# Holding back one load of V until the rows of the group before are scaled, with one attention schedule moved by a step

## The chip, the cores and the metric

The kernel runs on one core of a Trainium2 chip. The metric is device time in microseconds (us) of one launch. Engines are named as in the profile: PE (TensorE matmul), PEld (its weight loads), DVE (VectorE), ACT (ScalarE), POOL (GpSimd) and SP (SyncE, which issues transfers here).

## The reference

Linear attention without softmax, a root-mean-square norm on each head's rows, and then two dense products with an ELU between them:

```python
kv  = einsum('bhsd,bhse->bhde', k, v)            # q, k, v: (8, 8, 576, 64)
out = einsum('bhsd,bhde->bhse', q, kv)
rms = sqrt(mean(out * out, axis=-1) + 1e-06)
x   = (out / rms * g_norm)                        # as 4608 x 512
h   = x @ w_in                                    # 512 x 2048
g   = where(h > 0, h, exp(min(h, 0)) - 1)
y   = g @ w_out                                   # 2048 x 512, float32
```

## The kernel before, in words

**Groups.** The 4608 rows of x are worked on in nine groups T = 0 to 8 of 512 rows. A group is eight slots of 64 rows; a batch has nine such slots (`slot_of`), so that group T needs the attention of batches T - 1 and T, or of one of them. For each group PE makes the first product (`mm1`: eight tile pairs i = 0 to 7, 128 x 512 each half, contracted over four chunks c of x) and the second (`mm2_half`: four column blocks of rows, each in two halves of eight matmuls). The order of all instructions on every engine is the order in which the Python program emits them[...].

**ELU.** `elu` takes exp on ACT from PSUM (L350), then DVE makes min(e, 1) - 1 (L362) and the maximum or sum with h (L366). With `relu` set, ACT also writes Relu of h (L355), which frees the PSUM pair, and DVE adds from SBUF; tiles 3 and 5 of group 2 are made so.

**Attention of a group** (`attention`, names used in the schedule): `kv` multiplies K and V of the group's new batch (L156) and ACT copies the result to SBUF (L268). `se0` and `se1` make the rows of the two halves of the group (L250), each followed by a square on ACT (L277). `sum` sums the squares on DVE (L283), `inv` makes one over the root on ACT (L291, L292), and `mul` scales the rows into `xs` on DVE (L299) and has SP issue two DMA transposes of them into `xT` (L306). `gain` multiplies the transposed columns of that half by g_norm on DVE (L312). `kv`, `se0` and `se1` share one PSUM tile, `at`, so that each waits until the one before has been read: `se1` waits for `mul0`.

**Loads.** Q, K and V come by DMAs that POOL issues, K and V cast to bf16 on the way (L90). Q arrives in float32, POOL casts it (L103), and SP transposes it by DMA into `qT` (`turn_q`, L331). `after_turn` has POOL copy 16 elements of `qT` (L339), so that POOL's next loads are issued after that transpose has landed; `fetch_ahead(b)` then issues Q, K and V of batch b.

**Order around the change.** Ahead of the groups' code, POOL's program has the loads of batch 2, its casts, `after_turn(2)`, `fetch_ahead(3)` and the casts of batch 3. Group 1's first product then carries the attention of group 2 in it: `se0` and `se1`, `mul0` (first two L306) and `mul1` (other two). The second product of group 1 on two row blocks follows, then `gain0` and `gain1`, and group 2's first product begins: tile pair 0 is made in two halves of columns, 0:256 after `gain0`, 256:512 after `gain1`.

In groups 2 to 7 `window` runs over the eight tile pairs: after pair i's matmuls it emits `early[i]`, a half of the second product of group T - 1 if there is one for i, the ELU's DVE part, and `late[i]`. The pieces are those of the attention of group T + 1. Group 2's lists are:

```python
early = {2: ("sum0", "inv0"), 5: ("sum1", "inv1", "mul1"), 6: ("gain0",), 7: ("gain1",)}
late = {0: ("kv",), 1: ("se0",), 2: ("mul0",), 4: ("se1",), 5: ("ahead",)}
halves = {1: 5, 3: 6, 5: 7}
```

**Group 0** is made chunk by chunk as the loads come in. `early(tiles, c)` (L569) adds chunk c to the listed tiles (i, a) of the first three pairs; chunks come in the order 0, 2, 1, 3. Pair 0's PSUM is taken again by pair 4 of the same group, which thus waits for the ELU of pair 0.

Of the kernel before, what the change touches and what calls it, by code (L numbers as in the profile page):

```python
# [9 lines left out]
BF16 = mybir.dt.bfloat16  # L10
# [6 lines left out]
def kernel(  # L17
# [13 lines left out]
    nc = tc.nc  # L31
# [6 lines left out]
    J = 4  # L38
# [6 lines left out]
    const = ctx.enter_context(tc.tile_pool(name="const", bufs=1))  # L45
# [35 lines left out]
    def fetch(name, b, u=None):  # L81

        if (name, b) not in bf:
            bf[name, b] = qkvp.tile([P, 4, RK, D], BF16, name=f"{name}_bf", tag=name)
        ms = slice(0, 4) if u is None else slice(u, 4, 2)
        load(bf[name, b][:, ms], name, b, ms)

    def load(dst, name, b, ms=slice(0, 4), eng=nc.gpsimd):
        in_ = src_of[name][b].rearrange("h r d -> (h r d)").rearrange("(m p x) -> p m x", m=4, p=P)
        eng.dma_start(out=dst.rearrange("p m j d -> p m (j d)"), in_=in_[:, ms, :])  # L90

    def fetch_ahead(b):
        raw[b] = stage.tile([P, 4, RK, D], FP32, name="st_q", tag="q")
        load(raw[b], "q", b)
        for name in "kv":
            fetch(name, b)

    def cast_q(b):
# [27 lines left out]
    def at_tile():  # L126
        return ps_at.tile([P, 2, 512], FP32, name="at", tag="at")
# [19 lines left out]
    def x_tile(T):  # L147
        xT[T] = attp.tile([P, KC, G], BF16, name="xT", tag="xT")
        return xT[T]

    def kv_mm(b, kv_ps, u, ls=range(2)):
        for j in range(RK):
            for s in range(2):
                rows = slice(s * 64, s * 64 + 64)
                for l in ls:
                    nc.tensor.matmul(  # L156
                        kv_ps[s][l * 64 : l * 64 + 64, u * 64 : u * 64 + 64],
                        lhsT=bf["k", b][rows, 2 * l + u, j, :],
                        rhs=bf["v", b][rows, 2 * l + u, j, :],
                        start=(j == 0),  # L160
                        stop=(j == RK - 1),
                    )
# [78 lines left out]
    def se_mm(T, h, se_ps):  # L241

        for i in range(2):
            (b0, j0), (b1, j1) = (slot_of(T, 4 * h + 2 * i + t) for t in range(2))
            parts = [(0, P, b0, j0, 2)] if b0 == b1 else [(0, 64, b0, j0, 1), (64, P, b1, j1, 1)]
            for m in range(4):
                u, s = m // 2, m % 2
                for l in range(2):
                    for lo, hi, b, j, n in parts:
                        nc.tensor.matmul(  # L250
                            se_ps[lo:hi, l, (4 * i + m) * 64 : (4 * i + m) * 64 + 64],
                            lhsT=qT[b][l * 64 : l * 64 + 64, s, u, j : j + n, :],
                            rhs=kv_of(b, l, u, s),
                            start=True,
                            stop=True,
                        )

    def attention(T):

        st = {}  # L260

        def kv():
            if T == B:
                return
            kv_ps = at_tile()
            for u in range(2):
                kv_mm(T, [kv_ps[:, s, :] for s in range(2)], u)
            nc.scalar.copy(  # L268
                kv_sb[:, T], kv_ps[:, :, 0:P].rearrange("p s (u e) -> p u s e", u=2)
            )  # L270

        def se(h):
            def product():
                st["se", h] = at_tile()
                se_mm(T, h, st["se", h])
                sq = attp.tile([P, 2, DM], BF16, name="sq", tag="sq")
                nc.scalar.activation(sq, st["se", h], AF.Square)  # L277
                st["sq", h] = sq

            def sums():  # L280
                ss = attp.tile([P, 2 * H], FP32, name="ss", tag="ss")
                st["ss", h] = ss
                nc.vector.reduce_sum(  # L283
                    out=ss,
                    in_=st.pop(("sq", h)).rearrange("p l (m e) -> p (l m) e", e=D),
                    axis=AX.X,
                )

            def inv():
                ss = st["ss", h]  # L290
                nc.scalar.activation(ss, ss, AF.Ln, bias=eps_col, scale=1.0 / D)  # L291
                nc.scalar.activation(ss, ss, AF.Exp, scale=-0.5)  # L292

            def scale():
                if h == 0:
                    st["xs"] = attp.tile([P, J, DM], BF16, name="xs", tag="xs")
                    x_tile(T)
                se_ps, ss = st.pop(("se", h)), st.pop(("ss", h))
                nc.vector.tensor_tensor(  # L299
                    out=st["xs"][:, 2 * h : 2 * h + 2, :].rearrange("p i (l m e) -> p l i m e", l=2, e=D),  # L300
                    in0=se_ps.rearrange("p l (i m e) -> p l i m e", i=2, e=D),
                    in1=ss.rearrange("p (l i m) -> p l i m", l=2, i=2).unsqueeze(4).to_broadcast([P, 2, 2, 4, D]),
                    op=ALU.mult,
                )
                for i in (2 * h, 2 * h + 1):
                    nc.sync.dma_start_transpose(  # L306
                        out=xT[T][:, :, i * P : i * P + P], in_=st["xs"][:, i, :]
                    )

            def gain():  # L310
                cols = slice(2 * h * P, 2 * h * P + 2 * P)
                nc.vector.tensor_scalar(  # L312
                    out=xT[T][:, :, cols],
                    in0=xT[T][:, :, cols],
                    scalar1=g_col,
                    scalar2=None,
                    op0=ALU.mult,
                )

            return product, sums, inv, scale, gain  # L320

        pieces = {"kv": kv}
        for h in range(2):
            for name, piece in zip(("se", "sum", "inv", "mul", "gain"), se(h)):
                pieces[f"{name}{h}"] = piece
        return pieces
# [9 lines left out]
    def after_turn(b):  # L336

        gate = const.tile([1, 16], BF16, name="gate")
        nc.gpsimd.tensor_copy(out=gate, in_=qT[b][0:1, 0, 1, RK - 1, 0:16])  # L339
# [170 lines left out]
    cast_q(2)  # L510
    turn_q(2)
    after_turn(2)
    fetch_ahead(3)
    cast_q(3)

    nc.vector.memset(zeros, 0.0)
# [48 lines left out]
    def early(tiles, c):  # L565

        for i, a in tiles:
            h = h_ps[i]
            nc.tensor.matmul(  # L569
                h[a] if isinstance(h, list) else h[:, a, :],  # L570
                lhsT=w_in_sb[:, c, (2 * i + a) * P : (2 * i + a) * P + P],
                rhs=xT[0][:, c, :],
                start=(c == 0),
                stop=(c == KC - 1),
            )
# [66 lines left out]
    early([(0, 0), (0, 1), (1, 0), (1, 1), (2, 0)], 1)  # L642
    h_ps[2][1] = single("m", "h_ps")
    early([(2, 1)], 0)
    early([(2, 1)], 2)
    early([(0, 0), (0, 1)], 3)
    early([(2, 1)], 1)
    early([(1, 0), (1, 1), (2, 0), (2, 1)], 3)
    for i in range(3):
# [53 lines left out]
    at = attention(2)  # L703
# [23 lines left out]
    at["sum1"]()  # L727
    at["inv1"]()
    at["mul1"]()
    for i in (6, 7):  # L730
        freed[i]()
    for i in (6, 7):
# [35 lines left out]
    for T in range(2, NT):  # L768
        at, early, late = {}, {}, {}
        if T + 1 < NT:  # L770
            at = attention(T + 1)
            if T + 2 < B:
                cast_q(T + 2)

                def ahead(b=T + 2):
                    turn_q(b)
                    if b + 1 < B:
                        after_turn(b)
                        fetch_ahead(b + 1)
                at["ahead"] = ahead  # L780
            else:
                at["ahead"] = lambda: None
            early = {2: ("sum0", "inv0"), 4: ("sum1", "inv1"), 5: ("gain0",), 7: ("gain1",)}
            late = {0: ("kv",), 1: ("se0",), 2: ("mul0",), 3: ("se1",), 4: ("mul1", "ahead")}
        if T == 2:
            early = {2: ("sum0", "inv0"), 5: ("sum1", "inv1", "mul1"), 6: ("gain0",), 7: ("gain1",)}
            late = {0: ("kv",), 1: ("se0",), 2: ("mul0",), 4: ("se1",), 5: ("ahead",)}
        halves = {1: 5, 3: 6, 5: 7} if T == 2 else {0: 1, 1: 3, 2: 4, 3: 5, 4: 6, 5: 7}
        second = {i: (lambda n=n: mm2_half(T - 1, n)) for i, n in halves.items()}
        if T > 2:  # L790
            window(T, at, early, late, second)
        else:
            g_tile(T)
            opened = [pair("B", "h_ps")]
            mm1_part(T, 0, opened[0], range(KC), slice(0, 256))
            window(T, at, early, late, second, (3, 5), opened)
        mm2_half(T, 0)
        mm2_half(T, 2)
# [33 lines left out]
```

## Time and profile before

| | before |
|---|---|
| device time, three runs | 285.09, 285.09, 286.17 us; median 285.09 |
| the profiled execution | 286.17 us, of which its span is 284.4 |
| PE busy | 276.9 us, 97% of the span, 2123 matmuls |
| DVE, ACT, POOL busy | 58%, 50%, 17% |
| granted TensorE clock | 1.0 throughout |
| L306, transposes of the rows | 28, median 2.5 us to landing, longest 9.1 |
| L90, loads of V of a whole batch | 6, median 12.6 us to landing |

Spans and starts are in us from the first instruction of the profiled execution. A busy PE is not a PE at its peak: the ends of matmuls are modelled, and holes are better read from the distances between the starts. "Idle before, releaser" in a line is the time for which that engine stood still and what ended it. A DMA's line shows its issue; when its data has arrived is the time to landing.

### The profile page before, as it was taken

To read this page: it belongs to the slowest core of one execution; us is meant where nothing else is said; L and a number is where in the kernel's file an instruction comes from. 1 tells how busy PE (TensorE), PEld (TensorE's weight loads), DVE (VectorE), ACT (ScalarE), POOL (GpSimd) and SP (SyncE) were. 2 spreads that over 40 slices of the span, in tenths; PEclk is the share of its full clock that TensorE was granted. 3 is DMA by queue.
4 is the path that set the end of the run, shared out by engine and by line. 5 is a ranking of instruction groups with operands and counts; after the bars stand their busy time and mean duration, and the time that the engine had idled before them with its cause. 6 is when DMAs were issued, how large, how long until landed. Compare 5 with 4: busy or idle time off the path is not lost.

```text
span 284.4 us, 5154 instructions
## 1 busy us (share of the span) xinstructions
PE 276.9 (97%) x2123; PEld 129.1 (45%) x2123; DVE 164.4 (58%) x222; ACT 141.4 (50%) x209; POOL 47.9 (17%) x89
## 2 busy tenths in 40 slices
PE   8899999999899999999999999999999999999994
PEld 3444444444544444444444444444444444444443
DVE  2549532966487657754785378627863786344600
ACT  3778359594468255435542555345543554333311
POOL 7743303303330033033003120000000000000000
PEclk9999999999999999999999999999999999999999
DMA  7999999999896889779627971612150234020222
GB/s 208 198 203 207 206 263 236 174 298 144 191 282 72 163 182 239 94 176 262 148 37 172 248 173 35 157 37 74 37 113 0 74 39 111 0 76 0 74 74 75
DMA packets 50571, 39.46 MB, mean 139 GB/s; under 512 B 30964, under 2 KB 44020, under 8 KB 50548
## 3 DMA queue, kind: packets, MB, share of 16 engines
q0 software_dynamic: 15008, 21.30, 37.4%
q1 hardware_dynamic: 35136, 17.31, 29.4%
q10 hardware_dynamic: 404, 0.53, 0.5%
q8 instruction: 16, 0.26, 0.3%
q14 instruction: 7, 0.06, 0.1%
HBM read 36.70 MB, written 9.44 MB: 162 GB/s over the span
## 4 chain that ended last, share of the span: by engine, by line
PE 87%; DMA 6%; DVE 2%; ACT 2%; POOL 1%; issue 0%; SPq 0%; DVEq 0%; POOLq 0%
PE h_ps L382 40%; PE o_ps L403 40%; DMA xT<-xs 3%; DMA v_bf<-in_v_dram 3%; PE at L250 2%; PE at L156 1%; PE o_ps L440 1%; PE h_ps L569 1%; ACT elu_e L350 1%; DVE gT L366 1%; POOL k_bf L90 1%; PE mean L199 0%; PE qt_ps L174 0%; PE kv_ps L156 0%; PE y_ps L189 0%; DVE ss L283 0%
## 5 line engine op out<-in xcount | busy, mean ns | idle before, releaser
L403 PE MATMUL o_ps<-w_out_sb,gT 128*128 128x512 bf16 x560 | 129.7, 379 | 0.0
L382 PE MATMUL h_ps<-xT,w_in_sb 128*128 128x512 bf16 (+1 forms) x560 | 128.0, 376 | 1.0 <-DVE xT L312 0.9
L350 ACT ACTIVATE elu_e<-h_ps 128x1024 bf16<-128x1024 f32 (+1 forms) x79 | 74.0, 952 | 90.6 <-PE h_ps L382 89.0
L403 PEld LDWEIGHTS <-gT 128*128 128x128 bf16 x560 | 54.4, 98 | 65.8 <-issue 0.9
L382 PEld LDWEIGHTS <-w_in_sb 128*128 128x128 bf16 x560 | 53.2, 98 | 62.4 <-PE o_ps L403 1.4
L366 DVE TENSOR_TENSOR gT<-elu_e,h_ps 128x1024 bf16<-128x1024 bf16 (+1 forms) x67 | 77.2, 1157 | 6.9 <-PE h_ps L382 0.5
L362 DVE TENSOR_SCALAR elu_e<-elu_e 128x1024 bf16<-128x1024 bf16 x72 | 31.2, 433 | 64.6 <-ACT elu_e L350 64.6
L419 ACT COPY o_sb<-o_ps 128x512 f32<-128x512 f32 x32 | 18.3, 587 | 21.1 <-PE o_ps L403 21.1
L103 POOL CAST q_bf<-st_q 128x384 bf16<-128x384 f32 x36 | 16.8, 508 | 41.6 <-DMA st_q<-in_q_dram 41.6
L283 DVE TENSOR_REDUCE ss<-sq 128x16 f32<-128x1024 bf16 x14 | 17.1, 1220 | 6.8 <-ACT sq L277 6.8
L299 DVE TENSOR_TENSOR xs<-at,ss 128x1024 bf16<-128x1024 f32 x14 | 17.1, 1219 | 1.9 <-ACT ss L292 1.9
L277 ACT ACTIVATE sq<-at 128x1024 bf16<-128x1024 f32 x14 | 14.4, 1029 | 0.0
L212 DVE SCALAR_TENSOR_TENSOR xT<-y_ps,g_col,rT 128x512 bf16<-128x512 f32 (+1 forms) x10 | 6.2, 641 | 10.1 <-ACT rT L209 7.9
L339 POOL COPY gate<-qT 1x16 bf16<-1x16 bf16 x5 | 1.1, 217 | 59.0 <-DMA qT<-q_bf 59.0
L355 ACT ACTIVATE elu_h<-h_ps 128x1024 bf16<-128x1024 f32 (+1 forms) x12 | 9.3, 817 | 0.0
L156 PEld LDWEIGHTS <-k_bf 64*64 64x64 bf16 x576 | 6.4, 107 | 5.5 <-issue 5.5
L312 DVE TENSOR_SCALAR xT<-xT,g_col 128x1024 bf16<-128x1024 bf16 x14 | 6.7, 480 | 3.3 <-DMA xT<-xs 3.3
L90 POOL DMA_DIRECT2D v_bf<-in_v_dram x11 | 7.7, 700 | 4.2 <-DMA w_in_sb<-in_moe_w_in_dram 2.1
L90 POOL DMA_DIRECT2D k_bf<-in_k_dram x11 | 7.7, 704 | 2.6 <-DMA w_in_sb<-in_moe_w_in_dram 1.8
L250 PEld LDWEIGHTS <-qT 64*128 64x128 bf16 (+1 forms) x248 | 4.3, 97 | 6.1 <-issue 5.9
L112 DVE COPY o_sb<-o_ps 128x256 f32<-128x256 f32 x1 | 0.4, 424 | 11.1 <-PE o_ps L440 11.1
L366 DVE TENSOR_TENSOR gT<-elu_e,elu_h 128x1024 bf16<-128x1024 bf16 x9 | 6.2, 692 | 0.8
(57 smaller groups left out, 101.3 us busy)
## 6 DMA issues: line engine op xcount, KB each, us to landing
st_q<-in_q_dram POOLq DMA_DIRECT2D x6, 1152.0 KB, 8.4
out_dram<-o_sb SPq DMA_DIRECT2D x24, 256.0 KB, 3.4
k_bf<-in_k_dram POOLq DMA_DIRECT2D x6, 576.0 KB, 10.5
v_bf<-in_v_dram POOLq DMA_DIRECT2D x6, 576.0 KB, 12.6
out_dram<-o_sb SPq DMA_DIRECT2D x19, 128.0 KB, 2.4
w_out_sb<-in_moe_w_out_dram POOLq DMA_DIRECT2D x4, 512.0 KB, 15.4
w_in_sb<-in_moe_w_in_dram POOLq DMA_DIRECT2D x2, 512.0 KB, 10.7
q_bf<-in_q_dram POOLq DMA_DIRECT2D x3, 288.0 KB, 13.4
```

Of the source, the lines that this page charges most:

```text
L90: eng.dma_start(out=dst.rearrange("p m j d -> p m (j d)"), in_=in_[:, ms, :])
L103: nc.gpsimd.tensor_copy(out=bf["q", b][:, u, js], in_=raw[b][:, u::2, js, :].rearrange("p l j d -> p j l d"),)
L250: nc.tensor.matmul(se_ps[lo:hi, l, (4 * i + m) * 64 : (4 * i + m) * 64 + 64], lhsT=qT[b][l * 64 : l * 64 + 64, s, u, j : j + n, :], rhs=kv ...
L277: nc.scalar.activation(sq, st["se", h], AF.Square)
L283: nc.vector.reduce_sum(out=ss, in_=st.pop(("sq", h)).rearrange("p l (m e) -> p (l m) e", e=D), axis=AX.X,)
L299: nc.vector.tensor_tensor(out=st["xs"][:, 2 * h : 2 * h + 2, :].rearrange("p i (l m e) -> p l i m e", l=2, e=D), in0=se_ps.rearrange("p l ...
L350: nc.scalar.activation(e[:, lo:hi, :], h, AF.Exp)
L362: nc.vector.tensor_scalar(out=e, in0=e, scalar1=1.0, scalar2=1.0, op0=ALU.min, op1=ALU.subtract)
L366: nc.vector.tensor_tensor(out=gT[T][:, 2 * i + lo : 2 * i + hi, :], in0=e[:, lo:hi, :], in1=h, op=ALU.add if relu else ALU.max,)
L382: nc.tensor.matmul((ps[a] if isinstance(ps, list) else ps[:, a, :])[:, cols], lhsT=w_in_sb[:, c, f * P : f * P + P], rhs=xT[T][:, c, cols] ...
L403: nc.tensor.matmul(o_ps[T, j], lhsT=gT[T][:, f, j * P : j * P + P], rhs=w_out_sb[:, f, :], start=(f == 0), stop=(f == FC - 1),)
L419: nc.scalar.copy(o_sb[T, half][:, j % 2, :], o_ps[T, j])
```

## The change

It has three parts. `fetch_ahead(3)` issues Q and K alone; V of batch 3 is issued by POOL after `mul1` of group 2's attention, behind a copy of 16 elements of the `xs` that `mul1` writes (`held`). In group 2's window `kv`, `se0`, `sum0` with `inv0`, and `mul0` of group 3's attention come one tile pair later; the rest of the lists is as it was. In group 0, tiles (0, 0) and (0, 1) get chunk 3 ahead of tile (2, 1) getting chunk 2.

```diff
-    def fetch_ahead(b):
+    def fetch_ahead(b, names="kv"):
         raw[b] = stage.tile([P, 4, RK, D], FP32, name="st_q", tag="q")
         load(raw[b], "q", b)
-        for name in "kv":
+        for name in names:
             fetch(name, b)
...
-        pieces = {"kv": kv}
+        def held():
+
+            gate = const.tile([1, 16], BF16, name="gate")
+            nc.gpsimd.tensor_copy(out=gate, in_=st["xs"][0:1, J - 1, 0:16])
+
+        pieces = {"kv": kv, "held": held}
...
-    fetch_ahead(3)
+    fetch_ahead(3, "k")
     cast_q(3)
...
     early([(2, 1)], 0)
+    early([(0, 0), (0, 1)], 3)
     early([(2, 1)], 2)
-    early([(0, 0), (0, 1)], 3)
     early([(2, 1)], 1)
...
     at["sum1"]()
     at["inv1"]()
     at["mul1"]()
+    at["held"]()
+    fetch("v", 3)
     for i in (6, 7):
         freed[i]()
...
         if T == 2:
-            early = {2: ("sum0", "inv0"), 5: ("sum1", "inv1", "mul1"), 6: ("gain0",), 7: ("gain1",)}
-            late = {0: ("kv",), 1: ("se0",), 2: ("mul0",), 4: ("se1",), 5: ("ahead",)}
+            early = {3: ("sum0", "inv0"), 5: ("sum1", "inv1", "mul1"), 6: ("gain0",), 7: ("gain1",)}
+            late = {1: ("kv",), 2: ("se0",), 3: ("mul0",), 4: ("se1",), 5: ("ahead",)}
```

## The prediction

> **What bounds the kernel.** I read the page's chain first.
>
> ```profile
> PE 87%; DMA 6%; DVE 2%; ACT 2%; POOL 1%; issue 0%; SPq 0%; DVEq 0%; POOLq 0%
> ```
>
> PE sets the end. Neither edit removes a matmul, so only PE's idle time can be won or added. I therefore compared the starts of successive matmuls, which are 0.216 us apart when 512 columns wide. After the first 20 us there are only two holes besides the 0.10 us at each change to small tiles: 0.26 us at 21.48 and 1.10 us at 71.91. The waits from 69 to 74 us (total, times, longest) name the second:
>
> ```profile
> DVE xT L312 <- DMA xT<-xs: 2.6, 2, 2.2
> PE h_ps L382 <- DVE xT L312: 0.9, 1, 0.9
> ```
>
> The wait view shows 0.9 because it counts from the modelled end of a matmul. The chain (start, length) says what was late:
>
> ```profile
> 62.62 8.60 DMA xT<-xs
> ...
> 71.32 0.50 DVE xT L312
> ...
> 71.91 1.92 PE h_ps L382 x16
> ```
>
> The second of group 2's four row transposes (L306, call them T1 to T4) took 8.60 us. Time to landing of the four (first line), and of two at 147 to 149 us (second line), where no load is under way:
>
> ```profile
> DMA to landing us min/median/max: 4.0/6.7/9.1
> ```
> ```profile
> DMA to landing us min/median/max: 2.4/2.5/2.5
> ```
>
> What stood ahead of them, on POOL's timeline:
>
> ```profile
> 54.14 0.76 POOL L90 DMA_DIRECT2D v_bf<-in_v_dram  x1
> 64.01 2.76 POOL L103 CAST q_bf<-st_q 128x384 bf16<-128x384 f32 x6 [9.10 <-DMA st_q<-in_q_dram]
> 73.71 0.19 POOL L339 COPY gate<-qT 1x16 bf16<-1x16 bf16 x1 [6.95 <-DMA qT<-q_bf]
> ```
>
> Q, K and V of batch 3 are issued from 52.66. They land at 63.95, 67.47 and 70.72; T1 to T4 are issued at 61.37, 62.62, 66.93, 68.16 and land at 70.43, 71.23, 71.68, 72.16. Queues (packets, MB, share of 16 engines) from 63 to 65 us, then from 69 to 71 us:
>
> ```profile
> q0 software_dynamic: 367, 0.41, 118.6%
> q1 hardware_dynamic: 4, 0.01, 0.9%
> ```
> ```profile
> q1 hardware_dynamic: 614, 0.14, 143.9%
> q0 software_dynamic: 13, 0.01, 4.0%
> ```
>
> In the first stretch T1 and T2 are issued and yet nothing of theirs moves. In the second the last packets of V trickle through one slow engine, and the transposes hold all engines while moving 0.14 MB. So a transpose waits until a load ahead of it has left the slowest engine. The same is seen at 84.45 (T issued; V lands 88.21, T 88.83) and at 110.33 (V 116.11, T 116.62).
>
> **The Trainium skill.** "DMA: Bandwidth & Descriptors", Queues, rings and completion order: an engine takes turns between its queues packet by packet. This trace disagrees for transposes, which stood still behind q0 for over 2 us, so I use the trace. The same page, Latency and other measured facts: some engines are usually slower, and a load from GpSimd has its first byte after about 1 us. The trace agrees on the slow engine; here the first packet comes 1.48 to 2.62 us after POOL's issue (five loads of Q from 52.66 on). "Perfetto Trace Analysis", Summary: a DMA instruction's window hides the movement; hence landings are used here, not issue times.
>
> **Part 1, two matmuls earlier.** The matmuls of tiles (0,0), (0,1) with chunk 3 go ahead of (2,1) with chunk 2. PE reaches that place at 16.48 + 6 x 0.216 = 17.77. Chunk 3 is scaled at 16.88 + 0.88 = 17.76, plus 0.04 to the waiter: PE loses 0.03, and tile pair 0 is complete 0.19 sooner than its 18.60. ACT (18.62), DVE (19.68, 20.21) and the free pair, for which PE waits until 21.48, follow by 0.19. Gain: **0.19** of the hole of 0.26 (between 0 and 0.26). It comes to 71 us unchanged, since PE has no other hole between; W_out's last load (42.20) still lands before its first use at 42.67 - 0.19.
>
> **Part 2, V of batch 3 held.** Removed: V's issue at 54.14. Its 3.25 us (K to V landing) leave the queue ahead of T1 and T2. K still lands by about 67.5, T1 and T2 by about 68.3, so gain0 runs when DVE is free at about 69.0, before PE asks at 70.97 - 0.19 + 0.03 transition = 70.81. The whole hole of 1.10 is closed for the first half (8 matmuls of 256 columns, 0.87 us). The second half could start at 71.68 instead of 72.78, if gain1 is done. Before, gain1 ended at 72.75, just in time: **T4 is what is late next**.
>
> Added: a 1x16 copy on POOL (0.2 us, beside other work), then V. The copy waits for POOL's casts (66.77) and for DVE's second scaling (66.90 - 0.19 = 66.71), which is also what T3 waits for. Gate at 66.82, V's issue 0.54 later as at 73.71, i.e. 67.36; first packet at 68.8 to 70.0, I take 69.3. T3 is issued at 66.74, T4 at 67.97. A free transpose moves from 1.2 to 2.4 us after its issue, so T4 moves from 69.2 to 70.4: V arrives just ahead of it or among it. If T4 has to let V through, V needs 2.8 to 4.1 us (K to V landings of five batches), I take 3.2, and T4 comes 0.5 to 1.0 behind, I take 0.7: it lands at 69.3 + 3.2 + 0.7 = 73.2 (72.1 to 75.1). The second half starts 0.62 after that (72.16 to 72.78 before): 73.8. That is **+1.0** against 72.78 (0 to +2.9), although the first half began 1.1 sooner.
>
> Queued behind: on POOL the gate for qT of batch 3 and batch 4's Q, K, V. qT's two transposes (issued 69.53, 71.50) also move behind V, 1 to 2 us later, and so the loads of batch 4; these end near 90, their casts are wanted at 95.4 and their K and V at 99.8. Priced at nothing: 5 us of slack. SP's own order is unchanged.
>
> **Part 3, attention of group 3 a step later.** Moving kv, se0, sum0 and mul0 by a step costs PE no matmul, but se1 keeps its place after tile 4. All share one PSUM tile, so se1 must wait until mul0 has read se0's. The old timeline, PE, ACT, DVE:
>
> ```profile
> 83.69 1.89 PE L382 MATMUL h_ps<-xT,w_in_sb 128*128 128x512 bf16 x8
> 85.52 0.41 PE L250 MATMUL at<-kv_sb,qT 64*128 64x64 bf16 x16
> ```
> ```profile
> 83.09 1.02 ACT L355 ACTIVATE elu_h<-h_ps 128x1024 bf16<-128x1024 f32 x1
> ```
> ```profile
> 83.17 1.22 DVE L299 TENSOR_TENSOR xs<-at,ss 128x1024 bf16<-128x1024 f32 x1
> ```
>
> Before, mul0 ended at 84.39, 1.1 us ahead of se1. After, the scheduled order of DVE puts mul0 behind tile 3's add, which needs ACT's Relu. On the old clock: Relu ends 84.11, add starts 84.15, mul0 0.62 later at 84.77 and ends at 85.99; se1 is due at 85.52. New wait **+0.5** (0.3 to 0.7). Behind it PE holds tile 5 and everything after, so it is not given back. kv of group 3 itself, now due near 76.2 to 78.3, finds V landed (72.5 to 74.5).
>
> **Sum.** -0.19 is contained in the start of the first half. From 72.78 to 73.8 +1.0, and +0.5: **+1.5 us** on the profiled execution, 286.17 (its span 284.4 and 1.8 around it). The median shown is 285.09, 1.1 below it; carried over as a difference, 286.6. The profiled hole is as large as that 1.1, so shorter executions may have less to win; the upper end allows for it.
>
> **Rivals.**
> - *T4 gets through ahead of V* (ends not slower). The price is then just the new wait: second half at 71.68, -1.1 + 0.5 = -0.6: 284.5. It decides where V's first packet comes after 70.4, or T4's descriptors stand ahead on all engines. For it: after 124.49 and 153.88 Q's first packet came only 2.35 and 2.62 us later, with transposes in flight. Against: that would be 69.7 and 70.0 here, still among T4.
> - *V is late for kv too*: sharing with T3, T4 and qT it lands after 78, and PE waits at kv as well; +3, 288.1. Against: no V shown took over 4.1 us once K was in, and 78 is 9 us after its start.
> - *The wait only changes its name*: T4 lands near 72.2 as before, and the 0.5 at se1 is all that is new, or is itself hidden if Relu is early: 285.1 to 285.6.
>
> **Numbers.** About 0.5% (1.4 us) is what a measurement of this kernel can tell from no change. V ahead of T4: 0.60, 285.1 to 288.1 on its own, and about 0.33 of that over the bound; T4 ahead: 0.25, nearly all within the bound; V late: 0.08, over it; name only: 0.07, within. Over the bound 0.42, within 0.54, faster beyond it 0.04, as PE's two holes together are only 1.36. The range runs from the second case, 284.4, to the upper end of the first, 288.2.
>
> **What would show it.** Part 1: the matmul at 21.48 starts at 21.3. Part 2: T1 and T2 land by 68.5; PE's first 256-column matmuls start at 70.8 with no wait; after eight of them it waits on L312, L312 on xT, and T4 lands after V. If T4 lands before 71.1, the first rival holds. Part 3: PE waits about 0.5 us ahead of L250 near 86, on DVE's L299. I am wrong if V and transposes share the engines evenly, if V's first packet comes over 3 us after its issue, or if neither wait shows.

## The result, and the profile after

| | before | changed |
|---|---|---|
| device time, median | 285.13 us (four runs, 285.09 to 286.17) | 292.32 us (four runs, 291.43 to 292.98) |
| the profiled execution | 286.17, span 284.4 | 292.98, span 291.2 |
| mean granted TensorE clock | 1.0 | 0.986 |

The ratio of the mean times is 1.0241, with a 95% interval of 1.0202 to 1.028: 7 us slower, where 1.5 were predicted and 288.2 was the upper end. L306, L312, L156 and L250 keep their lines; `mm1` is now L387, `mm2` L408, `after_turn` L344 and `held` L325.

The page of the changed kernel: its PE and clock in 40 slices of 7.3 us, and the chain by engine.

```profile
PE   8899999998598999999999999999999999999994
PEclk9999999999689999999999999999999999999999
```
```profile
PE 78%; DMA 13%; DVE 4%; ACT 3%; issue 1%; POOL 1%; DVEq 0%; SPq 0%; POOLq 0%
```

PE has a hole in the eleventh slice, and TensorE's clock falls in that slice and the next. Waits from 70 to 78 us (total, times, longest), then the chain (start, length):

```profile
DVE xT L312 <- DMA xT<-xs: 5.7, 1, 5.7
PEld L387 <- issue: 4.3, 2, 3.8
PE h_ps L387 <- DVE xT L312: 4.1, 1, 4.1
```
```profile
68.25 7.12 DMA xT<-xs
...
75.46 0.50 DVE xT L312
75.96 0.04 issue
76.00 2.29 PE h_ps L387 x9
```

It is T4, the fourth row transpose, issued at 68.25, that PE waits for; L312 is `gain1`. What came between, on POOL's timeline:

```profile
67.12 0.25 POOL L325 COPY gate<-xs 1x16 bf16<-1x16 bf16 x1 [1.21 <-DVE xs L299]
67.63 0.75 POOL L90 DMA_DIRECT2D v_bf<-in_v_dram  x1 [0.26 <-ACT elu_h L360]
```

The queues (packets, MB, share of 16 engines) from 69 to 71 us:

```profile
q0 software_dynamic: 155, 0.18, 93.1%
q1 hardware_dynamic: 2, 0.00, 0.0%
```

V (q0) has the engines, and T4 (q1), issued only 0.6 us after V, moves nothing. V's first packet comes at 69.10 and V lands at 74.87; T4 lands at 75.37. T1 to T3 are no longer late: 66.18, 66.58 and 69.43. PE, on its timeline:

```profile
70.89 1.04 PE L387 MATMUL h_ps<-xT,w_in_sb 128*128 128x256 bf16 x8
76.00 2.29 PE L387 MATMUL h_ps<-xT,w_in_sb 128*128 128x256 bf16 x9 [4.07 <-DVE xT L312]
```

The first column half begins 1.02 us sooner than the 71.91 of before, and the second 3.22 later than its 72.78.

**The account** between the two profiled executions: second half 76.00 - 72.78 = 3.22. From there to the start of kv the changed kernel takes 83.22 - 76.00 = 7.22 us; the same matmuls at full clock took 4.41 (77.29 to 81.70, in the run with filling matmuls below): 2.81 for the clock. PE's wait ahead of se1 is 0.94 less the usual 0.10: 0.84. The sum is 6.87, against 291.2 - 284.4 = 6.8. Each of the two executions is the longest of its four; between the medians lie 7.2 us.

### The profile page after: what moved, and what is told of

Same layout as the page of the kernel before. It is cut to its first block, busy times and chain, and to the rows that moved or that the text cites. A ratio compares the mean times of both kernels' runs of the same rounds, so it can differ in the third digit from the quotient of the medians.

```text
span 291.2 us, 5123 instructions
## 1 busy us (share of the span) xinstructions
PE 277.9 (95%) x2089; PEld 130.5 (45%) x2123; DVE 164.4 (56%) x222; ACT 141.7 (49%) x209; POOL 49.0 (17%) x90
## 4 chain that ended last, share of the span: by engine, by line
PE 78%; DMA 13%; DVE 4%; ACT 3%; issue 1%; POOL 1%; DVEq 0%; SPq 0%; POOLq 0%
PE o_ps L408 37%; PE h_ps L387 36%; DMA w_out_sb<-in_moe_w_out_dram 5%; DMA w_in_sb<-in_moe_w_in_dram 3%; DMA xT<-xs 2%; DMA q_bf<-in_q_dram 2%; PE at L156 1%; PE at L250 1%; ACT elu_e L355 1%; DVE ss L283 1%; PE o_ps L445 1%; DVE xs L299 1%; DVE gT L371 1%; ACT sq L277 1%; DVE elu_e L367 0%
## 5 line engine op out<-in xcount | busy, mean ns | idle before, releaser
L387 PE MATMUL h_ps<-xT,w_in_sb 128*128 128x512 bf16 (+1 forms) x538 | 128.8, 382 | 5.3 <-DVE xT L312 4.1
L408 PE MATMUL o_ps<-w_out_sb,gT 128*128 128x512 bf16 x550 | 129.0, 380 | 0.8 <-issue 0.2
L408 PEld LDWEIGHTS <-gT 128*128 128x128 bf16 x560 | 54.6, 98 | 66.5 <-issue 1.9
L387 PEld LDWEIGHTS <-w_in_sb 128*128 128x128 bf16 x560 | 54.0, 99 | 66.4 <-issue 5.9
L103 POOL CAST q_bf<-st_q 128x384 bf16<-128x384 f32 x36 | 17.6, 531 | 39.8 <-DMA st_q<-in_q_dram 39.8
L299 DVE TENSOR_TENSOR xs<-at,ss 128x1024 bf16<-128x1024 f32 x14 | 17.1, 1219 | 2.7 <-ACT ss L292 2.7
L344 POOL COPY gate<-qT 1x16 bf16<-1x16 bf16 x5 | 1.1, 212 | 64.7 <-DMA qT<-q_bf 64.7
L312 DVE TENSOR_SCALAR xT<-xT,g_col 128x1024 bf16<-128x1024 bf16 x14 | 6.7, 480 | 6.4 <-DMA xT<-xs 6.4
L156 PEld LDWEIGHTS <-k_bf 64*64 64x64 bf16 x576 | 6.3, 107 | 5.2 <-issue 5.2
L250 PEld LDWEIGHTS <-qT 64*128 64x128 bf16 (+1 forms) x248 | 4.4, 97 | 6.8 <-issue 6.7
L250 PE MATMUL at<-kv_sb,qT 64*128 64x64 bf16 (+1 forms) x248 | 6.1, 193 | 0.8 <-DVE xs L299 0.8
```

Source lines behind the costliest of these rows:

```text
L103: nc.gpsimd.tensor_copy(out=bf["q", b][:, u, js], in_=raw[b][:, u::2, js, :].rearrange("p l j d -> p j l d"),)
L250: nc.tensor.matmul(se_ps[lo:hi, l, (4 * i + m) * 64 : (4 * i + m) * 64 + 64], lhsT=qT[b][l * 64 : l * 64 + 64, s, u, j : j + n, :], rhs=kv ...
L299: nc.vector.tensor_tensor(out=st["xs"][:, 2 * h : 2 * h + 2, :].rearrange("p i (l m e) -> p l i m e", l=2, e=D), in0=se_ps.rearrange("p l ...
L387: nc.tensor.matmul((ps[a] if isinstance(ps, list) else ps[:, a, :])[:, cols], lhsT=w_in_sb[:, c, f * P : f * P + P], rhs=xT[T][:, c, cols] ...
L408: nc.tensor.matmul(o_ps[T, j], lhsT=gT[T][:, f, j * P : j * P + P], rhs=w_out_sb[:, f, :], start=(f == 0), stop=(f == FC - 1),)
```

## The experiments

Theory 1: the held V is in the engines ahead of T4, PE waits, and the long wait makes the clock fall. Its rivals are named with each run. Each ratio is to the kernel before on the same chip, whose median was 285.0 to 285.4 us. A ratio takes in all executions of both kernels, so it can differ a little from the quotient of the medians. A wait "between starts" is the distance between the starts of two matmuls less the time that the first one needs. Dots in an edit stand for lines left out.

### The hold alone

The kernel before, with `fetch_ahead(3, "k")` and `held` followed by `fetch("v", 3)`; the window's lists and the first product as before.

> The kernel before with the hold of V alone; the schedule of group 2's window and the order of the first product are those of before. Theory 1 (the held V stands ahead of the last row transpose, PE's second column half waits some 4 us, and that long wait drops TensorE's clock): wait of 3.5 to 4.5 us on L312 near 72 us, clock at half for 6.8 us after it, no new wait at se1; 291.0 to 292.0, that is the changed kernel less about 0.8. Rival (the moved attention carries the loss): 285 to 287.

Measured: 290.76 us, ratio 1.0186 (1.0157 to 1.0215), just under what was expected. V lands at 74.59, T4 at 75.10, PE waits 4.15 us between starts, and the clock is 0.5 for 6.8 us. Its waits from 70 to 78 us, and two stretches of the wait (us; busy us of PE, PEld, DVE, ACT and POOL, each with the number of instructions; granted clock; DMA share; GB/s):

```profile
PE h_ps L387 <- DVE xT L312: 4.0, 1, 4.0
```
```profile
72.00:73.80 1.80, 0.00 (x0) 0.00 (x0) 0.00 (x0) 0.00 (x0) 0.00 (x0) 1.00 1.13 160
74.00:75.70 1.70, 0.00 (x0) 0.10 (x1) 0.48 (x1) 0.00 (x0) 0.00 (x0) 0.50 1.19 230
```

PE's last matmul ahead of the wait ends at 71.58, by the starts. The clock falls between 73.8 and 74.0, while PE still waits. The hold makes some 5.7 of the 7 us.

### The moved attention alone

```diff
-early = {2: ("sum0", "inv0"), ...
-late = {0: ("kv",), 1: ("se0",), 2: ("mul0",), ...
+early = {3: ("sum0", "inv0"), ...
+late = {1: ("kv",), 2: ("se0",), 3: ("mul0",), ...
```

> The kernel before with group 3's attention a step later in group 2's window, nothing else. Theory 1: one new wait of PE at L250 on DVE's L299, 0.5 to 0.8 us near 86 us, nothing else: 285.6 to 286.0. Rival (the moved attention carries the loss): 289 to 292. If the wait is taken up by slack later: 285.1.

Measured: 286.00, ratio 1.0036 (1.0020 to 1.0052). Waits from 80 to 90 us of this kernel:

```profile
PE at L250 <- DVE xs L299: 0.7, 1, 0.7
```

se1 waits for mul0, as predicted, and the time is not given back: 1.0 us. With the hold's 5.7 that makes 6.7 of the 7.2 us.

### The two earlier matmuls alone

```diff
+early([(0, 0), (0, 1)], 3)
 early([(2, 1)], 2)
-early([(0, 0), (0, 1)], 3)
```

> The kernel before with the two chunk-3 matmuls of pair 0 ahead of tile (2,1)'s chunk 2, nothing else. As predicted: the hole of 0.26 us at 21.48 closes and 0.15 to 0.2 us stays to the end: 284.9. Rival (a later wait takes it back: W_out's second quarter landed at 32.98 in the changed kernel, just as PE asked for it, and the row transposes before group 2 are set by DMA, not by PE): 285.1, no change.

Measured: 285.34, ratio 0.9998 (0.9984 to 1.0011): no change that can be seen. In its trace the hole of 0.26 us at 21.5 is closed, and PE waits 0.16 us more at 32.78 instead. The changed kernel's chain names the load that stands there:

```profile
17.58 15.41 DMA w_out_sb<-in_moe_w_out_dram
32.98 0.04 issue
33.03 0.38 PE o_ps L408
```

W_out's second quarter lands just as PE asks for it. This is the step "it comes to 71 us unchanged, since PE has no other hole": there was no hole, because PE came just late enough.

### Filling PE's wait

```diff
 mm1_part(T, 0, opened[0], range(KC), slice(0, 256))
+idle(18, at_tile()[:, 0, :])
```

> The changed kernel with 18 matmuls of zeros (3.9 us at full clock, written to the attention's PSUM tile, which is free then) between the two column halves of group 2's first tile pair, inside PE's wait. Theory 1 (the clock falls because PE stands still): clock 1.0 after the wait, about 2.7 us less than the changed kernel: 289.2 to 290.0. Rival (the low clock has another cause, or depends on useful work): still near 0.986 and 291.5 to 293.

Measured: 291.41, ratio 1.0196 (1.0160 to 1.0232), so the time was missed. The clock was not: its mean is 0.998 to 1.0 in all four executions. Stretches of the changed kernel, then of this one, in the columns named above:

```profile
76.00:80.00 4.00, 3.78 (x13) 2.07 (x14) 0.94 (x2) 1.02 (x1) 2.43 (x4) 0.50 1.03 227
```
```profile
76.00:80.00 4.00, 2.71 (x17) 1.75 (x18) 0.98 (x2) 1.02 (x1) 2.02 (x4) 1.00 1.09 236
```

In the changed kernel 13 matmuls begin in these 4 us. With filling the clock stays at 1.0, though the matmuls are of zeros. What took most of the gain back is T4: it landed 1.97 us behind V (76.65 against 74.68), where 0.50 was seen before. Between the two profiled executions the clock saves 2.81 us, the wait at se1 is 0.2 shorter, and the second half begins 1.29 later: 1.7 us are left (291.2 to 289.5). The queues from 73 to 75 us (the times of packets in flight together add up, so that a share can pass 100%):

```profile
q1 hardware_dynamic: 801, 0.20, 179.8%
q0 software_dynamic: 109, 0.11, 32.1%
q8 instruction: 1, 0.02, 3.4%
```

One packet of 16 KB of instructions came at this moment; it took 1.09 us on its engine, and until 76 the transposes held the engines with hardly a packet moving. In the changed kernel such a packet came at 77.1, when T4 had landed. That it came sooner here because of the added matmuls is likely, but was not tried apart.

### Half of V held

```diff
 fetch_ahead(3, "k")
+fetch("v", 3, 0)
...
-fetch("v", 3)
+fetch("v", 3, 1)
```

> The changed kernel, but only half of V of batch 3 (288 KB of 576) is held; the other half goes with K as before. Theory 1 with a slow start (the first load in an empty queue takes about 2 us to come up to speed, so V alone took 5.9 us from its first packet where 3.2 was priced): the held half takes 3.5 to 4.2 us, T4 lands at 73 to 73.8, PE waits 2 to 2.7 us there, [...] (1.0 throughout): 287.0 to 288.2. Rival (time in proportion to size): it takes 2.9 us, wait 1.0 to 1.6 us: 286.2 to 287. If the clock drops all the same: over 289.5.

Measured: 287.66, ratio 1.0091 (1.0077 to 1.0104). T4 lands at 73.00. Its waits from 70 to 76 us, and a stretch after the wait:

```profile
PE h_ps L387 <- DVE xT L312: 1.7, 1, 1.7
```
```profile
76.00:80.00 4.00, 3.95 (x87) 2.05 (x87) 3.04 (x4) 1.98 (x3) 1.24 (x2) 1.00 0.90 253
```

The wait, 1.89 us between starts, is less than half of the whole V's 4.24, and the clock stays at 1.0. First packet to landing is 3.31 us for the half and 5.77 for the whole. That lies between the two forecasts. A straight line through these two sizes, which is an estimate, gives a fixed part of some 0.9 us and 4.9 for a whole V at the held place, so a slow start alone hardly explains it.

### V still later, behind T4

```diff
 at["held"]()
+spare = const.tile([P, 3, 2, D], BF16, name="spare")
+for n in range(6):
+    nc.gpsimd.tensor_copy(out=spare, in_=raw[3][:, 0::2, 0:3, :].rearrange("p l j d -> p j l d"))
 fetch("v", 3)
```

> The changed kernel with six more casts on POOL (a part of Q to a spare tile, 2.8 us) between the gate and V's issue, so that V is issued near 70.4, after T4. Theory 1 (whoever is in the engines first goes first): T4 lands near 70.7, no wait of PE at the second column half, clock 1.0. V then lands at 76 to 78 and PE waits 0 to 1.8 us at kv, plus 0.8 at se1: 285.8 to 287.6. Rival (loads go ahead of transposes whatever their order, or T4 is late for another reason): T4 later than 73 and over 290.

Measured: 291.92, ratio 1.0234 (1.0217 to 1.0252). T3 and T4 to landing, the waits from 70 to 82 us, and the stretch after:

```profile
DMA to landing us min/median/max: 2.4/2.4/2.5
```
```profile
PE at L156 <- DMA v_bf<-in_v_dram: 3.8, 1, 3.8
```
```profile
80.00:86.00 6.00, 5.75 (x105) 2.93 (x107) 0.17 (x1) 1.60 (x3) 2.77 (x6) 0.50 1.13 284
```

T4 is free, as theory 1 says. V was issued at 71.24, as the six casts took 4.35 us, not 2.8; the two transposes of batch 3's Q, issued at 69.24 and 70.58, were in the engines first, and now V comes late: its first packet at 74.71, just after the first of them has landed (74.31), its landing at 79.89, and PE waits 3.93 us at kv, with the same fall of the clock. The time was outside what was expected, because only T4 had been thought of as standing in V's way. The queues from 72 to 74 us show one thing more:

```profile
q1 hardware_dynamic: 623, 0.15, 130.8%
q8 instruction: 1, 0.02, 2.9%
```

A packet of instructions came here too, and from 72.6 to 74 the transposes moved 88 packets only. That first transpose of Q took 5.1 us to land, as it did without V's load (next run), where such a packet came at the same time; it took 3.7 with the two matmuls alone moved, where the packet came behind it. So V did not start ahead of the first transpose, but how much of its delay is owed to the transposes, and how much to the packet, was not separated.

### Without V's load

```diff
-fetch("v", 3)
+bf["v", 3] = bf["v", 2]
```

> The changed kernel without the load of V of batch 3 (batch 2's V is used in its place); gate, schedule and order are kept. Theory 1 (V's transfer is what holds T4): T4 lands near 70.6, no wait at the second half, clock 1.0; only se1's wait of 0.8 is left: 285.6 to 286.2. Rival (the gate or the schedule holds it): 288 or more.

Batch 2's V is used in its place. Measured: 285.75, ratio 1.0025 (1.0015 to 1.0034). T3 and T4 to landing:

```profile
DMA to landing us min/median/max: 2.4/2.4/2.5
```

Gate, schedule and order are as in the changed kernel. So it is V's load that held T4.

The same in the kernel before, which then has no load of V of batch 3 at all:

> The kernel before without the load of V of batch 3 (batch 2's V is used in its place). It bounds what any later place of that load can win. If the hole of 1.10 us of the profiled execution is typical: 283.9 to 284.1. If it is not (most executions take 285.0, 1.1 below the profiled one, and two related runs profiled since had no such hole): 284.8 to 285.1, so that the hold had nothing to win.

Measured: 285.07, ratio 0.9996 (0.9987 to 1.0006). In the order of before, V's load of batch 3 costs nothing in most executions, so that no later place for it could win anything in them. None of the 13 executions without it took over 285.26 us, while 3 of the 22 of before took 285.8 or more; so the load may cost something in the long ones, but these are few.

### Before, once more

No edit.

> The kernel before once more, for a second profiled execution of it. If the hole of 1.10 us at 71.91 belongs to the rarer, longer executions alone: about 285.0 with span 283.2, T2 landing before 70.7 and no wait of PE on L312. If it is typical: the hole is there in an execution of 285.0 too.

Measured: 286.73 (span 284.9), again one of the long executions. Its waits from 69 to 75 us:

```profile
PE h_ps L382 <- DVE xT L312: 1.3, 1, 1.3
```

Between starts the hole is 1.46 us, and the first half begins at 72.49. The profiled execution of 286.17 had 1.10 and 71.91. In the runs with the two matmuls or the attention alone moved, which load V as before, it begins at 70.92 and 70.86 with no wait on L312. V lands at 70.72 and 71.29 in the two executions with the hole, and at 69.83 and 69.16 in these two without. Of the 35 executions of before beside the window's run, the median was 285.04 and five took over 286.2. No trace of before itself shows an execution of 285.0; that it has no such hole rests on these neighbours and on 284.4 - 1.1 = 283.3, the usual span.

### The two matmuls with W_out's quarter in halves

```diff
-for s in (1, 2):
-    load_w_out(s)
+load_w_out(1, 0, 2)
+load_w_out(1, 2, 4)
+load_w_out(2)
...
+early([(0, 0), (0, 1)], 3)
 early([(2, 1)], 2)
-early([(0, 0), (0, 1)], 3)
```

> The kernel before with the two chunk-3 matmuls moved as in the change and the second quarter of W_out loaded in two halves, the half that is used first ahead. If the 0.19 us that PE gains at 21.5 is taken back at 33 us by that load: the wait of 0.16 us there is gone and 0.15 to 0.2 us stays: 284.8 to 284.9. If something later sets the pace: 285.0.

Measured: 285.40, ratio 1.0006 (0.9990 to 1.0021). The wait at 33 us is gone, and another has come, on PE's timeline:

```profile
17.90 1.90 PE L570 MATMUL h_ps<-xT,w_in_sb 128*128 128x512 bf16 x8 [0.19 <-DMA w_in_sb<-in_moe_w_in_dram]
```

The earlier use of chunk 3 meets W_in's own load, in this execution. Whatever is left of 0.2 us lies below what this measurement can tell. No version tried beats the kernel before.

### V with no transpose behind it

```diff
 for i in (2 * h, 2 * h + 1):
+    if T == 2 and h == 1:
+        continue
     nc.sync.dma_start_transpose(
...
 fetch("v", 3)
+nc.gpsimd.memset(xT[2][:, :, 256:512], 0.0)
...
-turn_q(3)
-after_turn(3)
-fetch_ahead(4)
+qT[3] = qT[2]
```

Batch 4's loads and casts are issued after kv of batch 3.

> The disputed transfer by itself: the changed kernel, but behind the held V no transpose waits. T3, T4 and the transposes of batch 3's Q are left out (zeros and batch 2's transposed Q are used), and the loads of batch 4 come after kv of batch 3. If the transposes that wait in the engines slow V down: V lands 3.2 to 4.2 us after its first packet, near 72.2 to 73.2. Rival (a load that starts in an empty queue is slow by itself): 5 to 6 us, 74 to 75, as in the changed kernel.

Measured, from one trace: first packet 68.94, landing 73.76, so 4.82 us, between the two forecasts and nearer to the rival. The queue from 69 to 71 us, against 155 packets in the changed kernel:

```profile
q0 software_dynamic: 203, 0.23, 103.6%
```

By this one trace, about 1 of the 5.77 us is owed to the transposes that wait; the rest is V's own time where no other load is ahead of it. Why its packets are slow in the first 2 us was not settled.

## Why the prediction was wrong

- **Which mechanism.** The likeliest case named the delay: T4 is late next, behind V. The gate ran at 67.12 (66.82 predicted), V was issued at 67.63 (67.36), its first packet came at 69.10 (69.3), and T4 landed 0.50 behind V (0.7). T1 and T2 landed before 68.5, and PE's first half began at 70.89 (70.81). All these steps held.
- **The term that was too small.** "V needs 2.8 to 4.1 us, I take 3.2" came from the times between the landings of K and V. There V follows K in a full queue, and the time between two landings is not the time that V takes from its first packet. As the first load in the queue it took 5.77. T4 so landed at 75.37, not 73.2 and just above the upper end of 75.1, and the second half began at 76.00 instead of 73.8: +3.2 where +1.0 was taken.
- **The term that was missing.** The wait was priced at its own length only. A PE that stands still for long also loses its clock: 2.8 us more, unpriced in the case and in the range. The Trainium skill has it, in "TensorE: Matmul & The Clock Gate", What's actually happening: after an idle window of about 3.4 us the array's clock is halved. The runs agree that a long wait halves it: no fall with waits of 1.10, 1.46, 1.86 and 1.89 us, a fall to 0.50 with 3.93, 4.15 and 4.24, each for 6.83 us. They do not show 3.4 us as the edge: with the hold alone the clock fell 2.2 to 2.4 us after PE's last matmul, and no wait between 1.89 and 3.93 was measured. The prediction's own numbers lead into that gap and beyond it. From the end of its first half, 71.68, to its 73.8 is a wait of 2.1 us, and to its upper end, 75.72, one of 4.0; its "+2.9" counts from 72.78 and is not the wait.
- **The range.** On 285.09, the upper ends of its two terms, 2.9 and 0.7, make 288.7, so that 288.2 lay below its own terms. Both lie below the 292.3 measured; the clock's 2.8 us stand in no term.
- **Part 3.** The wait at se1 was there on L299, 0.84 instead of 0.5. Not ACT's Relu set it. From tile 2's min at 86.92 DVE works without a pause through tile 2's maximum, sum0 and tile 3's two operations to mul0 at 91.09; that sum0 (1.2 us) had moved in between was left out. The changed kernel's DVE:

```profile
88.83 1.21 DVE L283 TENSOR_REDUCE ss<-sq 128x16 f32<-128x1024 bf16 x1
89.96 0.42 DVE L367 TENSOR_SCALAR elu_e<-elu_e 128x1024 bf16<-128x1024 bf16 x1
90.48 0.69 DVE L371 TENSOR_TENSOR gT<-elu_e,elu_h 128x1024 bf16<-128x1024 bf16 x1
91.09 1.22 DVE L299 TENSOR_TENSOR xs<-at,ss 128x1024 bf16<-128x1024 f32 x1
```

- **Part 1.** PE's wait at 21.5 went, but the gain did not reach the end: loads for which PE had come just late enough took it back.
- **The base.** The hole of 1.10 us was read from one execution, one of the longer ones. The text said that shorter ones may have less to win; the run without V's load showed that most have nothing to win. Against the median the change could only lose.
- **The rivals.** T4 ahead of V: fell. V late for kv: not in this kernel (V landed at 74.87, kv began at 83.22), but in the run with V later still. The wait that only changes its name: fell.

## What to carry to other kernels

Price a transfer by the place that it will have: one that follows another in a full queue shows its throughput, not the time that it takes when it starts alone. When a wait of PE may come out longer than the 1.89 us that left the clock alone here, price the halved clock as well; half of the load held cost 2.7 us, the whole one 7. And before a wait is worked on, see whether the profiled execution stands at the median: a load whose removal changes nothing in most executions has no better place in them.

## What was not expected of the hardware

- A transpose issued 0.6 us after a load moved nothing for over 4 us, until the load was nearly through. A load issued 0.7 us after a transpose had its first packet 3.47 us after its issue, against 1.47 in the changed kernel, with a packet of instructions as a second possible cause.
- Each of the three falls of the clock lasted 6.83 us, and each began while PE still waited, with the hold alone 2.2 to 2.4 us after its last matmul.
- One 16 KB packet of instructions stood beside a delay of some 1.4 to 1.5 us of transposes in flight, in the run with filling matmuls and in the two where a transpose of Q took 5.1 us instead of 3.7.
